# Transposing the first batch's q by DMA and searching the order of all operations anew, in a fused attention and convolution kernel

## Chip, cores and metric

The kernel runs on one core of one Trainium2 chip. The metric is device time in microseconds (us) of one execution, as the median over runs. A run counts as slow when it is over 1.5% above the fastest run of the same kernel in the same measurement.

## The reference, cut to what matters

```python
# q, k, v: (8 batches, 8 heads, 576, 64); w_phi: (64, 128)
def phi(x):
    proj = einsum('bhsd,df->bhsf', x, w_phi)
    proj = proj - max(abs(proj), axis=-1)
    return concatenate([exp(proj), exp(-proj)], axis=-1)
q_p, k_p = phi(q), phi(k)
kv  = einsum('bhsf,bhsd->bhfd', k_p, v);  z = sum(k_p, axis=2)
x   = einsum('bhsf,bhfd->bhsd', q_p, kv) / einsum('bhsf,bhf->bhs', q_p, z)
# then, with x as (8, 576, 512) and w_proj: (512, 1536)
x1, x2, x3 = split(x @ w_proj)
y   = x1 * irfft(rfft(x2) * rfft(filter)) * x3
out = y @ w_out
```

## The kernel before

The kernel is one long list of words, `PLAN`. Each word is a method with its arguments and, behind `@`, the PSUM bank it works in. Every engine and every queue executes its words in the order of the list, each as soon as its inputs are there.

```python
for word in PLAN.split():
    name, _, bank = word.partition("@")
    self.bank = int(bank) if bank else None
    f, *args = name.split(",")
    getattr(self, f)(*[int(a) if a.isdigit() else a for a in args])
```

These methods are the ones that the change and the argument touch (bodies cut to their instruction):

```python
def load(self, n, b):            # k, q or v of batch b: 576 KB, issued by GpSimd
    self.nc.gpsimd.dma_start(out=self.at(n + "n", b)..., in_=self.dram[n][b]...)
def trh(self, n, b, X):          # half of k or q transposed by DMA, issued by SP
    self.nc.sync.dma_start_transpose(out=self.at(n + "T", b)[:, 9*X:9*X+9, :], in_=...)
def T(self, n, b, X, i):         # the same by TensorE, 8 tiles (i=0) or 1 (i=1) into PSUM
    for k in range(8 * i, 8 + i):
        self.nc.tensor.transpose(..., self.at("ident"))
def Te(self, eng, n, b, X, i):   # and out of PSUM, by ACT or DVE
    self.copy(eng, self.at(n + "T", b)..., self.turned(m))
def trm(self, b):                # mT: the maxima of q, transposed by DMA, issued by SP
    self.nc.sync.dma_start_transpose(out=self.at("mT", b), in_=self.at("mh", b)...)
def fold(self, eng, b, odd):     # sum or difference of the halves of x: eo, what X2 reads
    self.port(eng, self.elem(eng).tensor_tensor(out=self.at("eo", b)..., in0=x..., in1=x..., op=op))
...
def port(self, eng, first, last=None):   # GpSimd waits for the DVE words ahead of it so marked
```

For a batch the words are: `Pk`, `Qn` (projections of k and q), `max*`, `ex` and `em` (maxima, exp), `vs` (products with v), `KV`, `trm` (mT), `Pq` (projection of q less its maximum), `NE`, `rc`, `xn` (numerator, division), `trx`, `trxt` (x transposed by DMA; `trxt` is its tail), `fold`, `X1`, `X2`, `X3` (x @ w_proj), `F` (the DFT), `m1` to `m3` (product with the filter's), `I` (back), `ym`, `O` (w_out), `st`. `H` and `filt_*` make the filter's DFT once; `warm` fills TensorE with multiplications of zeros.

Of the kernel before, what the change touches and what calls it, by code (L numbers as in the profile page):

```python
# [24 lines left out]
zeros loadh,k,0,1 w_load,phi gen_rows gen_cols,0 gen_cols,1 gen_turns,ACT,0 gen_angles,0 loadh,k,0,0  # L25
gen_ident warm,10,4@0 T,k,0,1,0@0 loadh,q,0,0 warm,1,4@1 warm,7,1@1 T,k,0,0,1@1 gen_turns,ACT,1
gen_angles,1 T,k,0,1,1@2 Te,DVE,k,0,1,1@2 loadh,q,0,1 T,k,0,0,0@3 Te,DVE,k,0,0,0@3 gen_selidx
gen_pads load,v,0 load,k,1 gen_sin,0 Te,DVE,k,0,0,1@1 w_phi,ACT warm,2,4@4 warm,3,1@4 T,q,0,0,1@4
Te,DVE,k,0,1,0@0 gen_sin,1 warm,5,4@5 warm,2,1@5 Pk,0,0@2 maxk,0,0@2 warm,1,4@1 warm,3,1@1 Pkt,0@0
ex,k,p,0,0@2 maxkt,0@0 exkt,m,0@0 Pk,0,1@6 gen_sel gen_selx Te,ACT,q,0,0,1@4 load,q,1 maxk,0,1@6  # L30
em,p,0,0 T,q,0,0,0@5 exkt,p,0@0 Te,DVE,q,0,0,0@5 warm,2,4@4 warm,1,1@4 Qn,0,1@4 ex,k,m,0,0@2
gen_five maxq,0,1@4 Pk,0,3@0 maxk,0,3@0 em,m,0,0 vs,POOL,m,0,0 T,q,0,1,1@2 Te,DVE,q,0,1,1@2
T,q,0,1,0@3 ex,k,m,0,1@6 Te,ACT,q,0,1,0@3 vs,POOL,p,0,0 ex,k,p,0,1@6 ex,k,p,0,3@0 ex,k,m,0,3@0
Qn,0,0@4 maxq,0,0@4 Pk,0,2@2 maxk,0,2@2 em,m,0,1 Qn,0,2@6 maxq,0,2@6 Qnt,0@4 maxqt,0@4 w_load,proj,1
ex,k,p,0,2@2 ex,k,m,0,2@2 em,p,0,1 Qn,0,3@0 maxq,0,3@0 mhi,0 vs,POOL,m,0,1 mlo,POOL,0 filt_load,SP,0
filt_load,SP,1 filt_fold,POOL,2 KV,0,0@6 load,k,2 trh,k,1,0 Pk,1,0@4 trh,k,1,1 Pk,1,1@2 maxk,1,0@4
ex,k,m,1,1@2 trh,q,1,1 warm,2,4@0 Qn,1,2@0 ex,k,m,1,0@4 KVe,DVE,0,0@6 trh,q,1,0 maxk,1,1@2
ex,k,p,1,0@4 Qn,1,3@6 ex,k,p,1,1@2 maxq,1,3@6 maxq,1,2@0 vs,POOL,p,0,1 trm,0 Pq,0,0@4 ex,q,m,0,0@4
load,v,1 Qn,1,1@6 maxq,1,1@6 ex,q,p,0,0@4 Pq,0,1@2 filt_fold,POOL,1 ex,q,m,0,1@2 Qnt,1@0 maxqt,1@0
ex,q,p,0,1@2 Qn,1,0@4 maxq,1,0@4 w_load,proj,0 NE,0,0@6 rc,0,0@6 xn,0,0@6 Pq,0,3@0 ex,q,m,0,3@0  # L40
ex,q,p,0,3@0 filt_fold,POOL,0 Pkt,1@2 maxkt,1@2 em,m,1,0 KV,0,1@4 KVe,DVE,0,1@4 NE,0,1@6 mhi,1
rc,0,1@6 exkt,m,1@2 mlo,POOL,1 vs,POOL,m,1,0 load,q,2 xn,0,1@6 gen_fwd5 Pqt,0@0 exqt,p,0@0
exkt,p,1@2 NE,0,3@4 rc,0,3@4 xn,0,3@4 exqt,m,0@0 Pk,1,3@6 maxk,1,3@6 Pq,0,2@4 ex,q,m,0,2@4 H,4@2
NEt,0@0 H_ev,DVE,4@2 rct,0@0 xnt,0,1@0 ex,q,p,0,2@4 xnt,0,0@0 gen_fwd ex,k,p,1,3@6 ex,k,m,1,3@6
warm,2,4@3 Pk,1,2@2 maxk,1,2@2 NE,0,2@4 rc,0,2@4 xn,0,2@4 ex,k,m,1,2@2 H,1@0 H_ev,DVE,3@0 em,p,1,0
ex,k,p,1,2@2 H_ev,DVE,1@0 trx,0,0 H,0@6 H_ev,DVE,2@6 H_ev,DVE,0@6 trh,k,2,0 vs,POOL,p,1,0 gen_inv
trm,1 Pq,1,1@4 ex,q,m,1,1@4 H_fix late load,q,3 trx,0,3 trx,0,1 ex,q,p,1,1@4 Pq,1,0@0 ex,q,p,1,0@0
warm,3,4@2 warm,2,1@2 KV,1,0@2 KVe,ACT,1,0@2 Pk,2,1@6 trx,0,2 X1,0,1@4 ex,q,m,1,0@0 fold,DVE,0,0
em,p,1,1 NE,1,1@2 fold,DVE,0,1 X1e,ACT,0,1@4 trxt,0 foldt,DVE,0,0 foldt,POOL,0,1 rc,1,1@2 xn,1,1@2
em,m,1,1 vs,POOL,m,1,1 X2,0,1@5 X2e,DVE,0,1@5 X2,0,2@0 X2e,DVE,0,2@0 Pk,2,0@2 ex,k,p,2,1@6 X2,0,4@4  # L50
X2e,DVE,0,4@4 ex,k,m,2,0@2 maxk,2,1@6 vs,POOL,p,1,1 X2e,ACT,0,5@4 X2,0,3@5 X2e,ACT,0,3@5 X2,0,0@0
X2e,DVE,0,0@0 w_load,proj,2 ex,k,p,2,0@2 trh,k,2,1 maxk,2,0@2 load,v,2 ex,k,m,2,1@6 X1,0,0@4
X1e,ACT,0,0@4 warm,2,1@1 F,0,0@0 m1,0,0@0 Pqt,1@6 exqt,p,1@6 exqt,m,1@6 NE,1,0@2 trh,q,2,1 rc,1,0@2
xn,1,0@2 F,0,1@4 Fe,ACT,0,0@0 X1t,0@6 X1te,ACT,0@6 m1,0,1@4 Pkt,2@2 exkt,m,2@2 exkt,p,2@2
Fe,ACT,0,1@4 warm,2,1@7 Qn,2,3@0 maxq,2,3@0 warm,2,1@7 KV,1,1@6 maxkt,2@2 trh,q,2,0 KVe,ACT,1,1@6
load,k,3 em,p,2,0 Qn,2,1@0 m2,POOL,0,1 Pq,1,3@2 ex,q,p,1,3@2 m3,POOL,0,1 m2,POOL,0,0 maxq,2,1@0
Qnt,2@4 maxqt,2@4 ex,q,m,1,3@2 F,0,4@6 m1,0,4@6 Pq,1,2@0 ex,q,p,1,2@0 Qn,2,2@4 maxq,2,2@4 X1,0,3@7
X1e,ACT,0,3@7 m3,POOL,0,0 ex,q,m,1,2@0 Qn,2,0@2 maxq,2,0@2 mhi,2 X1,0,2@6 trx,1,1 X1e,ACT,0,2@6
mlo,POOL,2 Pk,2,3@4 maxk,2,3@4 em,m,2,0 X3,0,1@7 tm,0,1@7 Pk,2,2@0 ex,k,m,2,2@0 load,q,4 NE,1,3@2
rc,1,3@2 xn,1,3@2 trx,1,0 trh,q,3,0 vs,POOL,p,2,0 vs,POOL,m,2,0 X3t,0@6 tmt,0@6 X3,0,0@7 tm,0,0@7  # L60
ex,k,m,2,3@4 ex,k,p,2,2@0 NE,1,2@2 rc,1,2@2 trh,q,3,1 xn,1,2@2 ex,k,p,2,3@4 I,0,1,0@6 Ie,0,1@6
maxk,2,2@0 X3,0,3@7 I,0,0,0@2 Ie,0,0@2 em,p,2,1 em,m,2,1 load,k,4 vs,POOL,m,2,1 tm,0,3@7 I,0,0,1@3
NEt,1@4 trm,2 Pq,2,0@0 ex,q,p,2,0@0 ex,q,m,2,0@0 rct,1@4 xnt,1,1@4 xnt,1,0@4 Pq,2,1@6 ex,q,p,2,1@6
I,0,1,1@2 Ip,0,1@2 Im,0,1@2 X3,0,2@4 vs,POOL,p,2,1 Ip,0,0@3 I,0,2,0@5 trx,1,3 Im,0,0@3 warm,3,1@2
Qn,3,0@0 maxq,3,0@0 Ie,0,2@5 trx,1,2 warm,3,1@2 KV,2,0@2 tm,0,2@4 w_load,out ex,q,m,2,1@6 Qn,3,3@0
maxq,3,3@0 KVe,ACT,2,0@2 trh,k,3,0 fold,DVE,1,0 I,0,3,0@5 Ie,0,3@5 Pq,2,2@6 ex,q,m,2,2@6 NE,2,0@2
rc,2,0@2 xn,2,0@2 Qn,3,1@4 maxq,3,1@4 KV,2,1@0 ex,q,p,2,2@6 KVe,ACT,2,1@0 ym,POOL,0,1 Pk,3,0@2
ex,k,p,3,0@2 ex,k,m,3,0@2 Qn,3,2@6 maxq,3,2@6 X2,1,0@0 X2e,ACT,1,0@0 NE,2,1@4 rc,2,1@4 xn,2,1@4
X2,1,1@1 X2e,ACT,1,1@1 maxk,3,0@2 fold,POOL,1,1 Pq,2,3@6 Qnt,3@4 I,0,3,1@0 ex,q,p,2,3@6 ym,POOL,0,0
trh,k,3,1 X2,1,2@1 ex,q,m,2,3@6 X2e,ACT,1,2@1 maxqt,3@4 X2,1,3@2 trxt,1 foldt,POOL,1,0 foldt,DVE,1,1  # L70
X2,1,4@3 Im,0,3@0 load,v,3 load,k,5 Ip,0,3@0 X2e,DVE,1,3@2 trx,2,0 X2e,ACT,1,5@3 X2e,ACT,1,4@3
Pqt,2@6 exqt,m,2@6 I,0,2,1@1 Ip,0,2@1 ym,POOL,0,3 Im,0,2@1 exqt,p,2@6 ym,POOL,0,2 NE,2,3@4 mhi,3
mlo,POOL,3 F,1,0@2 Pk,3,1@0 ex,k,p,3,1@0 rc,2,3@4 xn,2,3@4 F,1,1@6 Fe,ACT,1,1@6 Fe,DVE,1,0@2
m2,POOL,1,1 O,0,1@4 Oe,ACT,0,1@4 X1,1,0@5 X1e,ACT,1,0@5 m1,1,0@2 NEt,2@2 m1,1,1@6 rct,2@2 xnt,2,1@2
xnt,2,0@2 ex,k,m,3,1@0 X1,1,1@4 m2,POOL,1,0 X1e,ACT,1,1@4 X1,1,2@5 X1e,ACT,1,2@5 Pkt,3@2 exkt,m,3@2
exkt,p,3@2 maxk,3,1@0 NE,2,2@6 rc,2,2@6 X1t,1@4 X1te,ACT,1@4 O,0,2@5 Oe,ACT,0,2@5 load,q,5
m3,DVE,1,0 maxkt,3@2 xn,2,2@6 em,m,3,0 O,0,0@0 Oe,DVE,0,0@0 Pk,3,3@2 maxk,3,3@2 Pk,3,2@4 F,1,4@1
ex,k,m,3,2@4 m1,1,4@1 X3t,1@0 ex,k,p,3,2@4 maxk,3,2@4 tmt,1@0 O,0,3@6 X3,1,1@7 tm,1,1@7 m3,POOL,1,1
X3,1,0@1 em,p,3,0 trh,k,4,0 vs,POOL,m,3,0 trh,q,4,0 ex,k,p,3,3@2 vs,POOL,p,3,0 ex,k,m,3,3@2 tm,1,0@1
I,1,1,0@4 Ie,1,1@4 I,1,1,1@5 Ip,1,1@5 trx,2,1 em,m,3,1 st,0,1 I,1,0,0@0 Ie,1,0@0 trm,3 Pq,3,0@2  # L80
load,v,4 I,1,0,1@4 trx,2,3 ex,q,m,3,0@2 ex,q,p,3,0@2 em,p,3,1 trx,2,2 fold,DVE,2,1 X3,1,2@7 tm,1,2@7
Im,1,0@4 X1,1,3@0 X1e,ACT,1,3@0 fold,POOL,2,0 st,0,0 I,1,2,0@1 trxt,2 Ip,1,0@4 I,1,3,0@7 Ie,1,2@1
Im,1,1@5 ym,POOL,1,1 ym,POOL,1,0 vs,POOL,m,3,1 Ie,1,3@7 KV,3,0@2 KVe,ACT,3,0@2 Oe,DVE,0,3@6
trh,k,4,1 st,0,3 Qn,4,1@0 maxq,4,1@0 Pq,3,2@4 ex,q,m,3,2@4 ex,q,p,3,2@4 I,1,3,1@6 X3,1,3@7 NE,3,0@0
Im,1,3@6 Ip,1,3@6 Pk,4,0@2 foldt,POOL,2,1 ex,k,m,4,0@2 rc,3,0@0 xn,3,0@0 X2,2,0@6 Pk,4,1@0 tm,1,3@7
X2e,ACT,2,0@6 I,1,2,1@4 ex,k,m,4,1@0 maxk,4,0@2 Ip,1,2@4 ex,k,p,4,1@0 trh,q,4,1 X2,2,3@5
X2e,DVE,2,3@5 X1,2,0@6 X1e,ACT,2,0@6 maxk,4,1@0 Im,1,2@4 X2,2,1@7 foldt,POOL,2,0 ex,k,p,4,0@2
trh,k,5,1 X2,2,2@5 X2e,ACT,2,2@5 X2,2,4@6 X2e,ACT,2,4@6 X2e,ACT,2,5@6 X2e,DVE,2,1@7 Qn,4,0@0
maxq,4,0@0 Pq,3,1@2 ex,q,p,3,1@2 ex,q,m,3,1@2 vs,POOL,p,3,1 KV,3,1@4 KVe,DVE,3,1@4 Pkt,4@6 F,2,1@0
exkt,p,4@6 trx,3,0 Fe,ACT,2,1@0 trh,k,5,0 Qnt,4@4 maxqt,4@4 maxkt,4@6 F,2,0@2 m1,2,0@2 exkt,m,4@6  # L90
ym,POOL,1,2 ym,POOL,1,3 m1,2,1@0 X1t,2@4 X1te,ACT,2@4 O,1,0@5 Fe,ACT,2,0@2 Pq,3,3@6 ex,q,m,3,3@6
ex,q,p,3,3@6 X1,2,1@4 X1e,ACT,2,1@4 st,0,2 Oe,DVE,1,0@5 NE,3,2@0 load,q,6 rc,3,2@0 xn,3,2@0 NE,3,1@2
rc,3,1@2 xn,3,1@2 st,1,0 O,1,1@5 NE,3,3@6 m2,POOL,2,0 Oe,ACT,1,1@5 m3,POOL,2,0 Pqt,3@0 exqt,p,3@0
rc,3,3@6 xn,3,3@6 em,p,4,0 F,2,4@4 m1,2,4@4 trx,3,2 Pk,4,3@2 ex,k,m,4,3@2 Qn,4,2@6 maxq,4,2@6
maxk,4,3@2 exqt,m,3@0 X1,2,3@5 X1e,ACT,2,3@5 trx,3,3 X1,2,2@4 Qn,4,3@0 maxq,4,3@0 Pk,4,2@6
# [915 lines left out]
```

## Time and profile before

| | before |
|---|---|
| median of 3 runs | 322.75 us (322.12 to 323.13) |
| TensorE (PE) busy | 290.9 us, 90% of the profiled span of 323.1 |
| first projection of q (batch 0) | 19.1 us |
| first use of mT of batch 0 | 39.1 us |
| first X2 of batch 0 / of batch 1 | 62.8 / 98.8 us |
| first F of batch 1 | 106.9 us |

In all views PE is TensorE and PEld its weight loads, DVE, ACT, POOL and SP are VectorE, ScalarE, GpSimd and SyncE. The granted clock is the share of TensorE's full clock that its throttle let through. An eviction copies a result out of PSUM, the memory that TensorE writes to.

The profile is read in stretches of time, since the front (up to some 105 us, where the first batches fill the pipeline) waits for data and the rest is bound by TensorE. The prediction below shows the stretches, the chain of waits and the single waits.

### The profile page before, as it was taken

What the parts mean: (1) busy time and instruction counts of PE and PEld (TensorE: products, weight loads), DVE (VectorE), ACT (ScalarE), POOL (GpSimd) and SP (SyncE); (2) the same over time, 40 slices, a digit from 0 to 9 for tenths busy, and PEclk for the clock granted to TensorE, in tenths of its full rate; (3) what the DMA queues carried; (4) which work ended last, traced back from release to release, by engine and by line L of the source; (5) the groups of instructions that cost most, each with busy time, mean ns of one, the idle gap of its engine ahead of it and who ended that gap; (6) DMA issues with size and microseconds to landing.
All of it is one profiled execution on the core that took longest, in us unless ns stands there. A gap on an engine that the chain in (4) does not pass through costs nothing.

```text
span 323.1 us, 9519 instructions
## 1 busy us (share of the span) xinstructions
PE 290.9 (90%) x3959; PEld 164.2 (51%) x3959; DVE 247.5 (77%) x409; ACT 232.3 (72%) x366; POOL 222.3 (69%) x174
## 2 busy tenths in 40 slices
PE   6755387999879999999999999999999999999981
PEld 2433263555555556555645655565475554654430
DVE  4697389589885897879788887898779877767850
ACT  5697197789677787988788776887877787434532
POOL 8849933379965788879769698847868668812230
PEclk9587589799997999999999999999999999999997
DMA  6999999999999999755995557267953222331416
GB/s 125 224 190 151 179 191 142 158 129 186 185 135 131 173 170 172 176 91 136 102 227 110 129 101 136 17 108 131 154 131 82 63 68 42 75 92 33 97 37 160
DMA packets 78667, 41.52 MB, mean 129 GB/s; under 512 B 58976, under 2 KB 73440, under 8 KB 78624
## 3 DMA queue, kind: packets, MB, share of 16 engines
q1 hardware_dynamic: 63808, 24.66, 43.4%
q0 software_dynamic: 14816, 16.25, 35.5%
q8 instruction: 31, 0.51, 0.7%
q14 instruction: 12, 0.10, 0.1%
HBM read 33.75 MB, written 9.44 MB: 134 GB/s over the span
## 4 chain that ended last, share of the span: by engine, by line
PE 74%; DMA 13%; SPq 4%; POOL 3%; DVE 2%; issue 1%; ACT 1%; POOLq 0%; DVEq 0%; ACTq 0%
PE ps L846 17%; PE ps L938 9%; PE ps L803 8%; PE ps L897 7%; DMA mT<-mh 7%; PE ps L460 6%; PE ps L711 5%; PE ps L732 5%; SPq L550 4%; DMA kn<-in_k_dram 3%; PE ps L623 2%; PE ps L617 2%; DMA xTt<-xnt 2%; PE ps L589 2%; PE ps L596 2%; PE ps L853 2%
## 5 line engine op out<-in xcount | busy, mean ns | idle before, releaser
L846 PE MATMUL ps<-xT,wproj 128*128 128x512 bf16 x256 | 63.9, 379 | 0.0
L656 DVE TENSOR_REDUCE mq<-ps 128x8 f32<-128x1024 f32 (+1 forms) x40 | 44.0, 1113 | 17.0 <-PE ps L596 14.4
L915 POOL TENSOR_TENSOR yT<-cv,x1s 128x576 bf16<-128x576 f32 x27 | 34.6, 1288 | 29.0 <-DVE cv L905 17.3
L656 DVE TENSOR_REDUCE mk<-ps 128x8 f32<-128x1024 f32 (+1 forms) x40 | 44.3, 1112 | 6.8 <-PE ps L589 4.4
L696 POOL TENSOR_TENSOR vm<-vn,vm 128x1152 bf16<-128x1152 bf16 x16 | 34.4, 2150 | 13.4 <-ACT vm L690 11.4
L640 ACT ACTIVATE Eqm<-ps 128x1024 bf16<-128x1024 f32 x32 | 32.8, 1026 | 13.9 <-PE ps L623 10.0
L696 POOL TENSOR_TENSOR vp<-vn,vp 128x1152 bf16<-128x1152 bf16 x16 | 34.3, 2146 | 7.7 <-ACT vp L690 5.7
L834 POOL TENSOR_TENSOR t<-C,B 128x1024 bf16<-128x1024 bf16 x15 | 31.8, 2122 | 10.5 <-ACT C L716 9.6
L938 PE MATMUL ps<-wout,yT 128*128 128x512 bf16 x144 | 36.0, 379 | 0.8 <-DVE yT L915 0.8
L640 ACT ACTIVATE Ekm<-ps 128x1024 bf16<-128x1024 f32 x32 | 32.5, 1028 | 5.0 <-PE ps L589 4.4
L897 PE MATMUL ps<-inv,Y 128*128 128x288 bf16 (+1 forms) x192 | 35.7, 289 | 0.0
L640 ACT ACTIVATE Ekp<-ps 128x1024 bf16<-128x1024 f32 x32 | 32.5, 1029 | 3.9 <-DVE mk L656 2.6
L640 ACT ACTIVATE Eqp<-ps 128x1024 bf16<-128x1024 f32 x32 | 32.5, 1023 | 3.7 <-PE ps L623 3.6
L846 PEld LDWEIGHTS <-wproj 128*128 128x128 bf16 x256 | 23.1, 98 | 23.5 <-issue 0.2
L803 PE MATMUL ps<-wproj,eo 128*128 128x512 bf16 x128 | 31.8, 387 | 0.0
L905 DVE TENSOR_TENSOR cv<-es,ps 128x288 f32<-128x288 f32 x64 | 26.1, 447 | 6.8 <-ACT es L900 3.0
L829 DVE TENSOR_TENSOR Y<-ps,A 128x1024 bf16<-128x1024 f32 (+1 forms) x24 | 24.8, 1043 | 6.9 <-PE ps L460 2.8
L839 POOL TENSOR_TENSOR Y<-Y,t 128x1024 bf16<-128x1024 bf16 x12 | 25.5, 2121 | 5.6 <-DVE Y L839 3.6
L716 ACT COPY o<-ps 128x512 f32<-128x512 f32 x27 | 15.7, 587 | 13.7 <-PE ps L938 11.1
L883 DVE TENSOR_TENSOR x1s<-ps,x1s 128x512 bf16<-128x512 f32 x32 | 21.7, 685 | 4.4 <-PE ps L846 3.9
L716 ACT CAST x1s<-ps 128x512 bf16<-128x512 f32 (+1 forms) x34 | 18.7, 552 | 7.0 <-PE ps L846 4.0
L716 ACT CAST x2n<-ps 128x512 bf16<-128x512 f32 (+1 forms) x32 | 16.2, 520 | 9.9 <-PE ps L803 7.3
(150 smaller groups left out, 640.8 us busy)
## 6 DMA issues: line engine op xcount, KB each, us to landing
out_dram<-o SPq DMA_DIRECT2D x72, 128.0 KB, 2.4
vn<-in_v_dram POOLq DMA_DIRECT2D x8, 576.0 KB, 8.1
kn<-in_k_dram POOLq DMA_DIRECT2D x7, 576.0 KB, 9.2
qn<-in_q_dram POOLq DMA_DIRECT2D x7, 576.0 KB, 8.5
wproj<-in_moe_w_proj_dram POOLq DMA_DIRECT2D x3, 512.0 KB, 8.0
fl<-in_moe_filter_fft_dram SPq DMA_DIRECT2D x18, 64.0 KB, 5.3
kn<-in_k_dram POOLq DMA_DIRECT2D x2, 288.0 KB, 5.3
qn<-in_q_dram POOLq DMA_DIRECT2D x2, 288.0 KB, 8.2
```

The costliest lines, as they stand in the source:

```text
L640: self.nc.scalar.activation(e, self.db(), AF.Exp, bias=0.0, scale=1.0 if g == "p" else -1.0)
L656: self.nc.vector.tensor_reduce(out=out, in_=src, axis=AX.X, op=ALU.max, apply_absolute_value=True)
L696: self.port(eng, self.elem(eng).tensor_tensor(out=t[:, :, :, 0:64], in0=self.at("vn", b)[:, 2 * X:2 * X + 2], in1=t[:, :, :, 64:65].to_bro ...
L716: self.nc.scalar.copy(dst, src)
L803: self.mm(self.pb(0), eo[:, kt, 128 * c:128 * c + 128], w[:, kt, 512:1024], start=(kt == 0), stop=(kt == 3))
L834: self.port(eng, self.elem(eng).tensor_tensor(out=self.at("t2", b)[:, t, :], in0=self.at("C", b)[:, o, :], in1=self.at("B"), op=ALU.mult))
L839: self.port(eng, self.elem(eng).tensor_tensor(out=Y, in0=Y, in1=self.at("t2", b)[:, i:i + 3:2, :], op=ALU.add if i else ALU.subtract))
L846: self.mm(self.pb(0), w[:, kt, f0 + 128 * m:f0 + 128 * m + 128], x[:, kt, :], start=(kt == 0), stop=(kt == 3))
L897: self.mm(self.pb(0, 0, 288), y, t, start=(k == 0), stop=(k == 2))
L905: self.nc.vector.tensor_tensor(out=self.at("cv", 4 * b + m)[:, :, odd, :], in0=e, in1=o, op=ALU.subtract if odd else ALU.add)
L915: self.port(eng, self.elem(eng).tensor_tensor(out=self.at("yT", b)[:, m, 0:SEQ], in0=self.at("cv", 4 * b + m).rearrange("p j h t -> p (j h ...
L938: self.mm(self.pb(0), y[:, kt, 128 * j:128 * j + 128], w[:, kt, :], start=first and kt == ks[0], stop=last and kt == ks[-1])
```

## The change

The intent: q of batch 0 is transposed by two DMAs in place of 18 TensorE transposes and four evictions, and the order of every word and the engine of every eviction, product and sum is the result of a new search that used queue times as measured on the chip. Only `PLAN` differs. The core of the diff, with cuts marked:

```diff
-zeros loadh,k,0,1 w_load,phi gen_rows gen_cols,0 gen_cols,1 gen_turns,ACT,0 gen_angles,0 loadh,k,0,0
...
-em,p,0,0 T,q,0,0,0@5 exkt,p,0@0 Te,DVE,q,0,0,0@5 warm,2,4@4 warm,1,1@4 Qn,0,1@4 ex,k,m,0,0@2
-gen_five maxq,0,1@4 Pk,0,3@0 maxk,0,3@0 em,m,0,0 vs,POOL,m,0,0 T,q,0,1,1@2 Te,DVE,q,0,1,1@2
-T,q,0,1,0@3 ex,k,m,0,1@6 Te,ACT,q,0,1,0@3 vs,POOL,p,0,0 ex,k,p,0,1@6 ex,k,p,0,3@0 ex,k,m,0,3@0
...
+ex,k,m,0,0@2 ex,k,p,0,0@2 Pk,0,3@6 em,m,0,0 maxk,0,3@6 trh,q,0,0 ex,k,m,0,1@4 warm,1,4@0 warm,3,1@0
+Qn,0,1@0 ex,k,p,0,1@4 maxq,0,1@0 trh,q,0,1 Qnt,0@2 maxqt,0@2 Pk,0,2@0 maxk,0,2@0 em,m,0,1 Qn,0,3@2
...
+xn,0,1@0 trx,0,1 em,p,1,0 NE,0,2@4 rc,0,2@4 xn,0,2@4 trx,0,2 Pk,1,3@0 maxk,1,3@0 ex,k,m,1,2@2
+ex,k,p,1,2@2 trxt,0 Pkt,2@4 exkt,p,2@4 exkt,m,2@4 em,m,1,1 Qn,2,0@2 maxq,2,0@2 Qn,2,1@2 ex,q,m,0,3@6
...
+trh,k,3,0 Qn,2,2@2 NE,1,1@4 maxq,2,2@2 fold,POOL,0,0 Pq,1,3@0 rc,1,1@4 xn,1,1@4 trx,1,1 ex,q,m,1,2@6
+NE,1,0@2 rc,1,0@2 xn,1,0@2 ex,q,p,1,2@6 NE,1,2@6 rc,1,2@6 xn,1,2@6 X2,0,0@4 mhi,2 late X2e,DVE,0,0@4
...
```

The last two hunks show: on TensorE, batch 2's projections (`Qn,2`), and batch 1's `NE`, now come ahead of batch 0's first `X2`. In the old order `X2,0` came soon after the first `NE` of batch 1.

## The prediction

> **What bounds the kernel now.** I read the profile in this order: engine busy times, the 40 slices, busy time by stretch, the chain of waits, then single waits and the issue times on the queues.
>
> The first view is the busy time of each engine in stretches of time (columns: stretch, its length, busy time of PE, PEld, DVE, ACT and POOL with instruction counts, granted TensorE clock, DMA share, GB/s).
>
> ```profile
> 0.00:20.00 20.00, 13.87 (x100) 7.07 (x101) 12.84 (x40) 13.17 (x22) 13.71 (x28) 0.83 0.97 183
> 20.00:40.00 20.00, 9.27 (x171) 7.04 (x172) 12.64 (x13) 11.12 (x17) 19.25 (x15) 0.64 1.19 163
> 40.00:60.00 20.00, 15.82 (x265) 9.83 (x262) 17.99 (x34) 15.88 (x22) 6.57 (x6) 0.85 1.18 168
> 60.00:80.00 20.00, 19.80 (x346) 11.38 (x344) 15.62 (x20) 17.20 (x28) 14.79 (x10) 1.00 1.23 153
> 80.00:100.00 20.00, 17.27 (x337) 11.36 (x336) 15.34 (x25) 14.62 (x23) 16.18 (x12) 0.93 1.26 161
> 100.00:300.00 200.00, 199.15 (x2673) 110.95 (x2672) 163.04 (x262) 151.59 (x244) 147.60 (x101) 1.00 0.65 113
> 300.00:323.10 23.10, 15.75 (x82) 6.58 (x79) 10.05 (x19) 8.70 (x16) 4.24 (x4) 0.92 0.44 103
> ```
>
> From 100 to 300 us TensorE is busy 199.15 of 200 us at full clock: that part is bound by TensorE, and no new order can shorten it. DVE is at 82% there and ACT at 76%. All that an order can win lies in the first 100 us (TensorE 76.0 us busy, that is 24 us idle, much of the rest at a granted clock of 0.64 to 0.85) and in the tail of 23 us, of which some 7 are eviction and store latency.
>
> The chain of waits (start, length, what; in order of time) says where the first 100 us go:
>
> ```profile
> 9.59 11.21 DMA kn<-in_k_dram
> ...
> 24.88 1.34 SPq L550
> 26.27 5.70 SPq L550
> 32.07 6.95 DMA mT<-mh
> ...
> 48.41 8.49 DMA mT<-mh
> ...
> 81.26 6.42 DMA mT<-mh
> ```
>
> These are transposes by DMA on the one SP queue. mT holds the maxima of q, which the feature map of q needs: no exp of q before it. For batch 0 its input was ready at 27.9 us (the end of the subtraction that makes mh), but SP was still issuing four half transposes of k and q of batch 1 (L550, from 20.8 us). It was issued at 32.07 and landed at 39.06. The quickest landing of any mT is 2.3 us. Batches 1 and 2 meet the same at 48.4 and 81.3 us. The waits by engine (total, times, longest, in the first 100 us) tell what that costs:
>
> ```profile
> PE ps L623 <- DMA mT<-mh: 8.0, 3, 4.3
> PE ps L596 <- DMA qT<-qn: 3.9, 1, 3.9
> ...
> ACT Eqm L640 <- PE ps L623: 7.8, 2, 7.2
> ```
>
> The idle TensorE is then clocked down, so the matmuls after a wait run slowly. The work that these waits hold back is ACT's (exp, 1.03 us for each 128x1024, eight a batch for q and eight for k) and DVE's (maximum, 1.22 us, half as many). The first projection of batch 0 starts only at 61.4 us.
>
> **What the Trainium skill says.** (1) "TensorE: Matmul & The Clock Gate", Part 1: the array runs at half rate until it has been busy for some 3.4 us, and goes back after an idle window. This trace agrees: 0.64 granted from 20 to 40 us, and the transposes of k take 271 ns against 223 for those of q. (2) "DMA: Bandwidth & Descriptors", Issuing engines are not separate DMA queues: DMAs of all issuers run on the same 16 engines. Agrees: the DMA slices read 9 almost without a break until 112 us, and a half transpose lands in 4.3 us (k) or 7.7 us (q), against a fastest of 2.8. (3) "Advanced Engine Details and Errata", X-Bar Transpose (TRN2): transposing DMAs are as fast as ordinary ones. The half load of q (288 KB) takes 8.2 us here and the half transpose of the same size 7.7, so nothing contradicts it; the cost is a place in the line, not the transposition.
>
> **The change, part by part.**
>
> *Removed:* 18 TensorE transposes of q. In the timeline they take 0.29 + 0.62 + 0.66 = 1.6 us in the first 21 us, where TensorE waits anyway. Their evictions are 1.00 + 0.27 us on ACT and 0.68 + 0.21 on DVE. Worth under 1 us on the path. *Added:* two half transposes of q by DMA at the head of the SP queue. q lands at about 13 to 14 us (issued at 4.5 and 5.3, some 8 us to landing), so with 4 to 5 us each (the four of before took (39.06 - 20.8)/4 = 4.6, mT included) the halves are there at about 18.5 and 22 us. Today the first q projection runs at 19.1 and the half of the last heads at 24.8. So this part alone is about even; it buys DVE and ACT time at the start for DMA time.
>
> *Engines:* counting the words of the two orders with the durations of the rows, the sums are ACT 253 against 255 us, DVE 262 against 264, TensorE's needed work 261 against 260, POOL 225 against 209 (these add overlapping latencies, so they stand 6 to 9% above the busy times). Work moves from POOL to DVE (two products, two sums and a fold of some 2.12 us each that cost DVE about 0.68), nothing is saved. Filling matmuls drop from 58 to 34. So a gain must come from waits.
>
> *Order, mT of batch 0:* before it SP now has six half transposes (q0, q0, q1, q1, k1, k1) and nine loads of the filter, but starts at about 14 instead of 20.8 us. 14 + 6 x 4.3 = 40 us, less what fewer competing loads give (the first part of w_proj and v of batch 1 now come later). I expect its landing at 37 to 41 us against 39.06: little gained. DVE and ACT have about as much behind them then (DVE 30 against 28, ACT 23.5 against 23 in sums). Gain 0 to 3 us, I take 1.5.
>
> *Order, mT of batches 1 and 2:* in the old order mT(1) stands behind a transpose of xn and one of k, and its use follows at once. In the new it is issued right after batch 0's first division, and between it and its use stand three more projections of q for batch 2, two for k of batch 1, all divisions of batch 0 and the sums of KV. mT(2) is issued before the first DFT of batch 0 and used after it and three projections. Today these cost TensorE 2.7 and 1.0 us of idleness, 1.6 us of filling, ACT 3.1 us before an exp of q. Most should go: 3 us.
>
> *Order, the rest:* a further 1.7 us of TensorE idle at 94.8 us and the clock of 0.87 from 90 to 100 us: 1 us. When batch 0 reaches its first X2, the new order has done NE of three parts of batch 1, all its Pq, and k and q of batch 2 partly; the old reaches the same TensorE sum (24 us) one X2 round later, at 66.4 us. ACT and DVE sums there are 2 to 4 us higher in the new, which takes back part: already netted in the above. *Tail:* 16 of the 20 last matmuls of w_out follow the last product, today 17; the ring of three output tiles still makes two evictions wait for a store. No change; the risk of 0.5 us either way. Shorter idleness also raises the clock earlier: 0.5 us.
>
> Sum: 0.8 + 1.5 + 3 + 1 + 0.5 = 6.8 us, so 322.75 - 6.8 = 316.0.
>
> **Rivals.** *ACT and DVE are the true bound of the front.* From 40 to 80 us they are busy 33.1 and 33.6 of 40 us; as all of that work stays, removing waits for mT moves the idleness elsewhere. For it: the sums above; against it: between 20 and 40 us both idle over 7 us, mostly for mT. It would give 319 to 322. *The DMA engines are the bound:* their slices are at 9 until 112 us, and the change adds two half transposes to them. Then mT(0) lands at 43 or later and the time is 321 to 325. Against it: the time in which a DMA is busy includes waiting in line, and up to 227 GB/s are moved in one slice against a mean of 161 here. *The search got it right:* it knew the queues' times, so mT(0) lands near 30 us and ACT no longer has its 7.2 us hole; with the 3 + 1 us above that gives 308 to 312.
>
> **Range and chances.** The second rival is unlikely, since an order that was searched with measured queues should not lose. The first and third are about equally likely and pull apart, so the range is wide: 309.5 to 321.5. The 2% line is at 316.3, next to my middle: faster 0.50, same 0.45, slower 0.05.
>
> **What would show it.** Right: TensorE idle for mT under 2 us in all; TensorE busy in the first 60 us above today's 39 us, or the same needed work in less; first X2 of batch 0 no later than 65 us with NE of batch 1 begun before; 100 to 300 us unchanged at over 99%. Wrong in the step of mT(0): landing after 42 us, or before 33. Wrong as a whole: if TensorE has new holes beyond 100 us, or DVE, which takes on POOL's work, is above 90% there and holds TensorE up.

## The result, and the profile after

The changed kernel took 341.92 us in the median of 4 runs (335.49 to 344.85), of which two count as slow; the kernel before took 322.94 beside it. The ratio is 1.046, with a 95% interval of 1.031 to 1.061: slower. Ratios here are the mean time of one kernel's fast runs over that of the other's in the same rounds, so not quite the ratio of the medians. Measured again as e0, the unchanged kernel gave 1.058 (1.047 to 1.070).

The busy times by stretch of the changed kernel (columns: stretch, its length, busy time of PE, PEld, DVE, ACT and POOL with instruction counts, granted TensorE clock, DMA share, GB/s):

```profile
0.00:20.00 20.00, 11.17 (x73) 4.73 (x73) 15.76 (x43) 14.32 (x22) 12.39 (x29) 0.85 0.98 171
20.00:40.00 20.00, 8.21 (x164) 6.43 (x166) 11.82 (x12) 8.64 (x14) 10.02 (x7) 0.55 1.06 176
40.00:60.00 20.00, 9.77 (x214) 7.47 (x211) 11.52 (x18) 11.92 (x17) 10.23 (x9) 0.71 1.23 182
60.00:80.00 20.00, 14.80 (x314) 9.64 (x311) 14.66 (x23) 13.84 (x21) 14.24 (x12) 0.84 1.08 132
80.00:100.00 20.00, 18.22 (x172) 8.65 (x171) 14.28 (x21) 16.80 (x28) 3.17 (x5) 0.94 1.28 184
100.00:300.00 200.00, 198.61 (x2830) 112.72 (x2830) 166.69 (x269) 152.78 (x243) 147.94 (x99) 1.00 0.64 112
```

(The DMA share is the summed time of the packets over that of 16 engines; packets overlap, so it can pass 1.) From 100 to 300 us hardly anything changed. From 20 to 80 us, taken together, every engine is less busy than before, TensorE with 8.21, 9.77 and 14.80 us in place of 9.27, 15.82 and 19.80, at a lower granted clock. No engine became the bound; all wait more.

The chain of waits of the changed kernel (start, length, what):

```profile
5.27 8.18 DMA qn<-in_q_dram
13.47 1.81 SPq L548
15.38 7.49 SPq L548
...
36.69 7.76 DMA mT<-mh
...
54.21 5.60 DMA qT<-qn
...
74.97 3.43 issue
...
89.03 9.85 DMA xT<-xn
99.62 0.68 DVE eo L785
...
118.02 2.37 PE ps L458 x12
```

q of batch 0 has landed by 13.47 us and its transposes are issued at once, but issuing the second keeps SP (L548) until 22.9 us, and the two halves land only at 26.9 and 27.9 us. mT of batch 0 is issued at 36.69 and lands at 44.45 (before: 32.07 and 39.02). The later waits for mT are gone from the chain, and waits for qT and xT stand in their place. The last line is the first F of batch 1: it comes 11 us later than before, where the same view has

```profile
107.04 1.18 PE ps L460 x6
```

That line settles where the loss lies. The last matmuls of TensorE are in the timeline (start, length, what; before first)

```profile
312.74 3.86 PE L938 MATMUL ps<-wout,yT 128*128 128x512 bf16 x17 [0.85 <-DVE yT L915]
...
323.53 3.31 PE L936 MATMUL ps<-wout,yT 128*128 128x512 bf16 x14 [0.35 <-DVE yT L913]
```

so they end at 316.6 and 326.8 us. From this F (in the timeline: 106.88 us before, 117.86 after) to that end it is 209.7 us before and 209.0 after. The whole loss of the profiled run, 11 us, lies ahead of it.

And it isn't more work. These are TensorE's busy time up to that F and, in the second line of each pair, the part of it that is filling (`warm`); before first:

```profile
0.00:106.88 106.88, 82.88 (x1286) 50.46 (x1287) 79.03 (x139) 77.14 (x115) 73.69 (x74) 0.86 1.16 163
...
0.00:106.88 106.88, 14.77 (x58) 5.69 (x58) 0.86 1.16 163
```

```profile
0.00:117.86 117.86, 78.81 (x1241) 47.25 (x1242) 84.12 (x140) 78.28 (x120) 65.69 (x71) 0.81 1.06 163
...
0.00:117.86 117.86, 10.64 (x34) 3.53 (x34) 0.81 1.06 163
```

82.88 - 14.77 = 68.1 us before, 78.81 - 10.64 = 68.2 us after: the needed work is the same, and it takes 11 us longer to get through. In the four stretches of 20 us up to 80 us (the same views, filling taken off) TensorE is busy with needed work for 1.4, 0.6, 3.8 and 4.6 us less than before: most of the lag arises from 40 to 80 us, after q of batch 0 is there. The waits of TensorE in those 117.86 us (total, times, longest):

```profile
PE ps L594 <- DMA qT<-qn: 9.9, 2, 9.1
PE ps L601 <- DMA kT<-kn: 3.8, 2, 3.1
PE ps L594 <- DVE mq L654: 3.6, 3, 1.4
PE ps L621 <- DMA mT<-mh: 3.5, 1, 3.5
...
PE ps L801 <- DVE Y L827: 2.7, 1, 2.7
```

The wait for mT fell from 8.0 to 3.5 us, as the change meant it to. But qT rose from 3.9 to 9.9, and kT (3.8), the maxima (3.6, before 0.2) and DVE (2.7) are new.

### The profile page after: what moved, and what is told of

Read it like the earlier page. It is cut to its first block, busy times and chain, and to the rows that moved or that the text cites.

```text
span 333.7 us, 9450 instructions
## 1 busy us (share of the span) xinstructions
PE 287.3 (86%) x3917; PEld 161.4 (48%) x3917; DVE 251.2 (75%) x414; ACT 232.7 (70%) x367; POOL 206.5 (62%) x164
## 4 chain that ended last, share of the span: by engine, by line
PE 72%; DMA 10%; SPq 7%; DVE 3%; ACT 2%; issue 2%; POOL 1%; DVEq 0%; POOLq 0%; ACTq 0%
PE ps L844 16%; PE ps L895 9%; PE ps L801 8%; PE ps L936 8%; PE ps L458 6%; SPq L548 6%; PE ps L730 5%; PE ps L709 5%; DMA xT<-xn 3%; DMA qn<-in_q_dram 2%; DMA mT<-mh 2%; PE ps L615 2%; PE ps L587 2%; PE ps L594 2%; PE ps L621 2%
## 5 line engine op out<-in xcount | busy, mean ns | idle before, releaser
L694 POOL TENSOR_TENSOR vm<-vn,vm 128x1152 bf16<-128x1152 bf16 x16 | 34.4, 2154 | 32.1 <-DVE eo L785 17.3
L913 POOL TENSOR_TENSOR yT<-cv,x1s 128x576 bf16<-128x576 f32 x26 | 33.0, 1278 | 19.1 <-DVE cv L903 10.1
L832 POOL TENSOR_TENSOR t<-C,B 128x1024 bf16<-128x1024 bf16 x13 | 27.6, 2123 | 20.0 <-ACT C L714 17.7
L594 PE MATMUL ps<-wphi,qT 64*128 64x128 bf16 x256 | 15.2, 242 | 14.4 <-DMA qT<-qn 9.9
L714 ACT COPY o<-ps 128x512 f32<-128x512 f32 x30 | 17.8, 593 | 13.9 <-PE ps L936 11.3
L714 ACT CAST x2n<-ps 128x512 bf16<-128x512 f32 (+1 forms) x34 | 17.1, 503 | 12.1 <-PE ps L801 9.7
L730 PE MATMUL ps<-KVs,Eqm 128*128 128x65 bf16 x256 | 20.7, 197 | 3.4 <-issue 3.4
```

Of the source, the lines that this page charges most:

```text
L694: self.port(eng, self.elem(eng).tensor_tensor(out=t[:, :, :, 0:64], in0=self.at("vn", b)[:, 2 * X:2 * X + 2], in1=t[:, :, :, 64:65].to_bro ...
L714: self.nc.scalar.copy(dst, src)
L730: self.mm(self.pb(u, c, c + 65), E.rearrange("f i t -> f (i t)"), KVs[:, u, v, s, :], start=(s == 0), stop=(s == 1))
L832: self.port(eng, self.elem(eng).tensor_tensor(out=self.at("t2", b)[:, t, :], in0=self.at("C", b)[:, o, :], in1=self.at("B"), op=ALU.mult))
L913: self.port(eng, self.elem(eng).tensor_tensor(out=self.at("yT", b)[:, m, 0:SEQ], in0=self.at("cv", 4 * b + m).rearrange("p j h t -> p (j h ...
```

## The experiments

Eighteen runs, all with correct results, each timed in 3 rounds. Nine of them change the new order a little, one the old one a little, two are the kernel itself or the part undone, and six join the two orders or move larger pieces.

One regularity holds through them. In 19 of the 20 profiles (these and the two of above) the time from the first F of batch 1 to the end of TensorE's last matmul is 208.6 to 209.7 us (e11: 213.2). (The expectation of e15 calls it 205.8 us, which is the time to the start of the last group of matmuls.) So the start of that F is the time of the kernel less a constant, and it is given with each run as F1. Landmarks in the tables are of the profiled run, which was slow in e1, e2, e5, e15 and e16; no conclusion rests on those alone.

### Is it the transposes of q? e0, e1, e2, e3

e0 is the changed kernel once more. e1 keeps the new order and gives q of batch 0 back to TensorE; e2 keeps the old order and takes q by DMA; e3 is the changed kernel with the loads behind q held back.

```diff
 e1 (new order)
-trh,q,0,0   -trh,q,0,1
+T,q,0,0,1@1 Te,ACT,q,0,0,1@1 T,q,0,0,0@0 Te,DVE,q,0,0,0@0        (behind maxk,0,3)
+T,q,0,1,1@3 Te,DVE,q,0,1,1@3 T,q,0,1,0@2 Te,ACT,q,0,1,0@2        (behind maxq,0,1)
 e2 (old order)
-T,q,0,*  -Te,*,q,0,*
+filt_load,SP,0 filt_load,SP,1 trh,q,0,0 trh,q,0,1                (the filter's loads moved ahead)
 e3 (new order)
+  load,q,1 waits for the maximum of part 3 of k (about 18.5 us); load,k,1 and load,v,0, moved
+  up beside it, and load,k,2 come behind it on the same engine
```

Expected of e0:

> The changed kernel unchanged, on the same chip as the other three. All theories: 335 to 345 us. It tells how wide its own runs spread (335.5 to 344.9 in the first four) next to those of the kernel before.

Of e1:

> The changed kernel with its own order, but q of batch 0 transposed by TensorE again (18 transposes and 4 evictions put in where q lands). Theory A (the two half transposes of q stood in the DMA line behind 2.3 MB of loads and held everything back): first q projection at 16 to 20 us instead of 27, mT of batch 0 lands by 40 us instead of 44.5, time 325 to 331 us. Theory B (the rest of the new order lost the time, the transposes are harmless): first q projection early too, but the time stays at 335 to 342 us.

Of e2:

> The kernel before with its own order, only q of batch 0 transposed by DMA (the filter's loads stay ahead of it on SP, where they in fact ran). Theory A: the halves take over 8 us to land, first q projection at 23 us or later instead of 19.1, time 326 to 332 us. Theory B: 321 to 325 us, as before.

Of e3:

> The changed kernel with the loads of q1, k1, v0 and k2 held back until the fourth part's maximum of k is taken (about 18 us, today issued at 8.2 to 11 us). Theory A: with the DMA engines free, both halves of q land within 6 us of their issue (by 20 us instead of 27) and the first q projection runs by 20 us; the time gains little or nothing since batch 1 now comes late: 328 to 338 us. If the halves still take over 10 us, the loads are not what they stood behind, and theory A falls.

| | median (range), us | ratio to before | first projection of q | mT(0) used | F1 |
|---|---|---|---|---|---|
| before (same rounds) | 323.34 (317.37 to 325.73) | 1 | 19.1 | 39.1 | 106.9 |
| e0 | 338.32 (336.28 to 349.74) | 1.058 (1.047 to 1.070) | 26.9 | 44.0 | 120.1 |
| e1 | 343.88 (336.84 to 345.03) | one fast run, 336.84 | 20.1 | 40.5 | 126.6 |
| e2 | 339.18 (330.07 to 342.97) | one fast run, 330.07 | 27.3 | 48.7 | 125.7 |
| e3 | 341.49 (341.33 to 345.87) | 1.075 (1.059 to 1.091) | 17.6 | 50.4 | 123.3 |

Over the mean of the three fast runs of before, 319.0 us, the two single fast runs are 1.056 (e1) and 1.035 (e2), worked out by hand and without an interval.

Two things follow. The half transposes wait for the loads beside them: the two queues of the changed kernel from 13 to 18.5 us (packets, MB, share of 16 engines), and the issue line of the two halves (how many, median us to landing), read

```profile
q0 software_dynamic: 975, 1.09, 115.4%
q1 hardware_dynamic: 154, 0.04, 5.3%
...
qT<-qn SPq DMA_TRANSPOSE x2, 13.0
```

and the same stretch of e3, where no load is under way, reads

```profile
q1 hardware_dynamic: 2368, 0.59, 47.5%
...
qT<-qn SPq DMA_TRANSPOSE x2, 2.9
```

Four loads issued by GpSimd between 8.2 and 11.7 us (q and k of batch 1, v of batch 0, k of batch 2) take the engines, and the transposes get 0.04 of 1.13 MB. Without them a half takes 2.9 us in place of 13.0. This cause of q's late start is shown. But it is not the whole loss: e1 has q at 20.1 us and is as slow as e0, and e3 has it at 17.6 us and is slower, because the held loads bring batch 1 late (TensorE waits 13.1 us for its qT) and mT of batch 0 behind it on SP.

So in the old order the new way to transpose q loses some 3.5% by itself (one fast run), and in the new order undoing it wins nothing (again one fast run). The two parts of the change don't add up: each of them alone reads slower than the kernel before.

### Is it the bursts of loads? e5 to e8

In the changed kernel v, v, k and q of batches 2 to 4 are issued together at about 80 us, and the transposes of x of batch 1 then take 9.85 us (the chain above). e5 moves three of these loads behind the products of batch 2; e6 is e5 with q by TensorE; e7 and e8 also part the first burst, with q by TensorE and by DMA.

```diff
 e5
+vs,POOL,m,2,0 load,v,3 load,k,4 load,q,4         (the loads from their places further up)
 e6 = e5 with the edit of e1
 e7 = e6 and
+vs,POOL,p,0,1 load,q,2
+filt_fold,POOL,0 load,k,3 w_load,proj,1
+trm,0 filt_load,SP,0
 e8 = e7 without the edit of e1
```

Expected of e5, e6, e7 and e8:

> The changed kernel, only three loads (v3, k4, q4), which it issues together with v2 at 80 to 83 us, put behind the first product of batch 2 on GpSimd, which waits for the fold of batch 1. Theory A2 (transposes on the SP queue starve behind bursts of loads on the GpSimd queue, wherever the order makes a burst): the last transposes of xn of batch 1 land within 5 us instead of 9.9, the fold of batch 1 and its X2 come 5 to 8 us earlier, time 328 to 333 us. Theory B2 (the order loses elsewhere, the burst is chance): 336 to 342 us.

> The same with q of batch 0 by TensorE as well: both places mended. Theory A2: in the run with q by TensorE alone the gain at the start was eaten at the second burst (16 us for the transposes of xn), so with both mended the two gains add: 320 to 327 us. If it stays over 333 us, something else in the new order sets its time.

> As the last, and in addition the burst of four loads around the first mT (q2 at 35.7, v1, k3 and part of w_proj at 40.8 to 43 us) taken apart: q2 behind two products, k3 and w_proj behind the folding of the filter, and the second half of the filter's loads behind mT on SP. Theory A2: mT of batch 0 lands by 37 us, q2's transposes no longer wait, time 312 to 322 us, below the kernel before. Theory B2: no better than the last.

> All the loads spread as in the last, but q of batch 0 by DMA as in the change. With the last, the changed kernel and the one with q by TensorE alone it makes a two by two. Theory A2: the transposes of q still stand behind the loads of q1, k1 and v0, so it is 5 to 12 us slower than the last: 322 to 332 us. If it is equal to the last, the move of q to DMA costs nothing by itself.

| | median (range), us | ratio to before | mT(0) used | F1 |
|---|---|---|---|---|
| before (same rounds) | 321.53 (319.72 to 333.95) | 1 | | |
| e5 | 349.23 (344.3 to 357.25) | 1.081 (1.062 to 1.099) | 44.2 | 139.1 |
| e6 | 347.28 (344.81 to 349.6) | 1.083 (1.072 to 1.094) | 39.0 | 127.8 |
| e7 | 345.04 (342.99 to 346.91) | 1.076 (1.065 to 1.086) | 36.6 | 124.6 |
| e8 | 349.24 (347.94 to 350.25) | 1.089 (1.083 to 1.095) | 40.7 | 131.3 |

None came near the 312 to 333 us that the theory of the bursts (A2) foretold for them. All four read slower than the changed kernel (1.046 and 1.058 in other rounds; the interval of e7 overlaps that of e0). e6 shows one reason in one line, the longest wait of its TensorE between 60 and 140 us (the X2 of the tail of batch 1, for the sum of that tail):

```profile
PE ps L807 <- POOL eo L794: 11.8, 1, 11.8
```

The SP queue is executed in order. With the load of k of batch 4 moved back, its transpose waits for the load at the head of SP, and the transpose of batch 1's tail, which needs nothing more, stands behind it: it is issued at 108.6 us. e5, e7 and e8 carry the same wait (11.4, 9.5 and 11.2 us), so these four are no clean trial of the bursts; e9 and e11 below are. e7 and e8, which differ in the transposes of q alone, are 4.2 us apart in the mean of their fast runs (5 to 12 were expected); e5 and e6, which do too, are level. mT(0) at 36.6 us in e7, the earliest of all, brought nothing in the end: what is gained there is lost later.

### Is it the place on the SP queue? e9 to e12

e9 is e6 with the tail of batch 1 moved to right behind its last part. e10 takes e1 and puts batch 0's last part and its tail ahead of k and q of batch 2 on SP; e11 is both; e12 is e10 with q by DMA.

```diff
 e9 = e6 and
+trx,1,3 trxt,1
 e10 = e1 and
+ex,q,p,0,3@6 ex,q,m,0,3@6
+trx,0,2 NE,0,3@6 rc,0,3@6 xn,0,3@6 trx,0,3
+trxt,0 trh,k,2,0 trh,k,2,1 trh,q,2,0 trh,q,2,1
 e11 = e10 with e5 and e9;   e12 = e10 without the edit of e1
```

Expected of e9 to e12:

> The kernel with q by TensorE and the second burst split, with one more move: the transposes of batch 1's tail (xTt) ahead of the transposes of k of batch 4 on the SP queue. In the run before they waited on SP behind a transpose whose load had just been put later, and TensorE stood 11.8 us for the fold that needs them. Theory C (what costs is the order on the in-order SP queue: a transpose that is needed now stands behind one that is needed later or not yet loaded): that wait goes, 332 to 338 us. Theory A2 (bursts alone) would expect nothing more: 343 to 349 us.

> The new order with q of batch 0 by TensorE, and batch 0 finished first: the last NE of batch 0 and all four transposes of its xn go ahead of the transposes of k and q of batch 2 on SP and ahead of the projections of batch 2 on TensorE. Nothing else is moved. Theory C: fold of batch 0 by 61 us instead of about 70 to 73, first X2 by 64 us, time 326 to 336 us. Theory A2: no gain, since the loads are where they were: 337 to 345 us.

> Both of these together with the second burst split. Theory C: the gains add, 316 to 328 us, around the kernel before. If it stays above 335 us, theory C is not the main term either.

> Batch 0 first as above, with q of batch 0 by DMA as in the change. Theory C with A as a second term: 6 to 12 us slower than the same with q by TensorE, as the first q projection is at 27 us again. If the two are equal, the transposes of q cost nothing once the order is mended.

| | median (range), us | ratio to before | first X2 of batch 0 | F1 |
|---|---|---|---|---|
| before (same rounds) | 323.28 (321.91 to 326.18) | 1 | 62.8 | 106.9 |
| e9 | 339.27 (338.45 to 341.98) | 1.050 (1.039 to 1.061) | 82.0 | 121.8 |
| e10 | 337.34 (334.65 to 340.45) | 1.040 (1.029 to 1.051) | 83.7 | 121.2 |
| e11 | 339.82 (336.05 to 342.7) | 1.046 (1.035 to 1.057) | 81.8 | 117.5 |
| e12 | 342.10 (339.67 to 344.99) | 1.055 (1.045 to 1.065) | 83.2 | 122.1 |

SP in e6 and, last line, in e9 (start, length, what):

```profile
106.48 2.02 SPq L550 DMA_TRANSPOSE kT<-kn  x1
108.59 1.40 SPq L775 DMA_TRANSPOSE xTt<-xnt  x1
...
94.69 1.17 SPq L775 DMA_TRANSPOSE xTt<-xnt  x1
```

e9 confirms the head of the queue: the tail is issued at 94.7 us, the wait of 11.8 us is gone, and the time falls from 1.083 (e6, other rounds) to 1.050 of before, 8 us between the medians and 10 by the ratios; 332 to 338 us were expected. With the wait gone, the split of the second burst still wins nothing: e9 is at 1.050 where e1 without it had 1.056 (one fast run), and e11 at 1.046 where e10 has 1.040. So theory A2 falls. e10 and e12 differ in the transposes of q alone: 1.040 against 1.055, so these cost some 4.8 us of the median there (6 to 12 were expected), though the intervals still overlap. e10 also has a miss: the four parts of x of batch 0 are issued by 56.3 us, and the first X2 of batch 0, foretold by 64 us, comes at 83.7. In the list it still stands behind the words of batches 1 and 2. e11 decides on theory C (the order on SP): it was to give 316 to 328 us, and to fall as the main term above 335. It took 339.8.

### Which stretch of the order loses? e13 to e15

Here the two orders are joined. e13 has the words of the old order up to the end of the filter (some 60 us) and then the rest in the new order; e14 has the new order, with q by TensorE, up to the first X2 of batch 0 and then the old; e15 has the old order up to the first X2 of batch 1 (99 us) and then the new. Readers of a bank that the cut left open were taken along.

Expected of e13, e14 and e15:

> The order of the kernel before, q of batch 0 by TensorE, up to the end of the filter (some 60 us), all that is left in the order of the changed kernel. If the new order loses in its first 60 us (theory A): 320 to 326 us, F of batch 1 starting by 112 us. If it loses between 60 and 107 us, by holding X2 of batch 0 behind projections of batch 2 whose q and k are still being transposed (theory B): 332 to 342 us, TensorE idle for qT or kT for over 6 us between 60 and 85 us, first X2 of batch 0 after 72 us.

> The order of the changed kernel with q of batch 0 by TensorE up to its first X2 of batch 0, all that is left in the order of the kernel before. Under A and under B alike the loss is in the front, so F of batch 1 comes after 115 us and the time is 332 to 342 us. If the loss came only after the first X2 of batch 0 (theory C: loads of v, k and q in one burst at 80 us), it would be 320 to 328 us.

> The order of the kernel before up to the first X2 of batch 1 (some 99 us), then the order of the changed kernel. If the new order is as good as the old from there on, as the equal 205.8 us from F of batch 1 to the end say: 320 to 326 us, F of batch 1 by 110 us. If its later part also loses: over 328 us. A gain over the kernel before (under 319 us) is not expected.

| | median (range), us | ratio to before | first X2 of batch 0 | of batch 1 | F1 |
|---|---|---|---|---|---|
| before (same rounds) | 320.78 (318.73 to 323.61) | 1 | 62.8 | 98.8 | 106.9 |
| e13 | 335.31 (333.79 to 336.68) | 1.047 (1.039 to 1.054) | 75.6 | 99.3 | 118.1 |
| e14 | 340.99 (339.0 to 342.71) | 1.065 (1.058 to 1.072) | 82.0 | 118.9 | 125.8 |
| e15 | 331.62 (326.93 to 333.57) | 1.027 (1.016 to 1.038) | 62.8 | 103.4 | 115.8 |

Theory A, that the new order loses in its first 60 us, would have made e13 as fast as before; it falls as the only cause. e13 is level with the old order until 60 us (q at 18.5, mT(0) at 38.8) and then loses nearly as much as the whole change. Its two stretches after that are

```profile
60.00:80.00 20.00, 14.20 (x244) 10.13 (x238) 13.00 (x18) 11.12 (x16) 13.39 (x13) 0.66 1.07 127
80.00:100.00 20.00, 14.40 (x145) 7.20 (x146) 12.92 (x20) 13.60 (x25) 1.19 (x1) 0.93 1.24 191
```

against 19.80 and 17.27 us of TensorE before. But theory B, that X2 stands behind batch 2's qT and kT, had foretold 6 us of idleness for these, and there is none between 60 and 85 us. What its TensorE waits for there is GpSimd's product for batch 1's KV (2.8 us) and the maxima (1.4), and from 60 to 80 us it runs at a clock of 0.66. e15 has a miss too: 320 to 326 us were expected, and the joint at 99 us costs 2.7% as well, all of it ahead of F1. e14 fell in the range that both theories gave it. A joined order is one that nobody searched, so part of a loss after a joint may be the joint's own: these runs narrow the place down, and don't prove it.

### What in that stretch? e16, e17, e18

e16 changes e10: batch 2's projections of q and of the tail of k, their maxima and mT go behind X2 of batch 0, and the sums of batch 0 go to DVE. e18 does the same to e13, with one part of k of batch 2 as well, and leaves the sums. e17 changes e13 the other way about: batch 0's x out at once, its sums on DVE, and its X2 ahead of KV of batch 1 and all of batch 2, as in the old order.

```diff
 e16 = e10 and
+X2e,ACT,0,4@1 Pkt,2 exkt,*,2 maxkt,2 Qn,2,* maxq,2,* Qnt,2 maxqt,2 mhi,2 mlo,POOL,2 trm,2
-fold,POOL,0,*   +fold,DVE,0,0 fold,DVE,0,1                   (behind NE,1,1)
 e17 = e13 and
+trx,0,2 trxt,0 trh,k,2,1 trh,q,2,0 trh,q,2,1
+fold,DVE,0,* foldt,DVE,0,* X2,0,0 X2,0,1 X2,0,2 X2,0,3 X2,0,4 (each with its eviction)
 e18 = e13 and
+X2e,ACT,0,4@1 Pkt,2 ... Qnt,2 maxqt,2 mhi,2 mlo,POOL,2 trm,2 Pk,2,3 maxk,2,3 ex,k,*,2,3
```

Expected of e16, e17 and e18:

> e10 with the projections of q of batch 2 and of the tail of its k, their maxima and mT moved behind X2 of batch 0, and the sum and difference of batch 0 on DVE in place of GpSimd. Under B the first X2 of batch 0 starts at 68 to 75 us in place of 84, and the time falls from e10's 337 to 325 to 332 us. If something else holds that X2 (the filter, or ACT's exps of batch 1), it still starts after 78 us and the time stays at 334 to 340.

> e13 with one thing changed: the last transposes of batch 0's x issued at once, its sum and difference on DVE, and X2 of batch 0 placed ahead of KV of batch 1 and of all of batch 2 on TensorE, as the kernel before has it. If the new order loses by leaving TensorE nothing to do while batch 1's products (exp, product on GpSimd) are made: first X2 at 62 to 67 us, F of batch 1 by 113 us in place of 118, 325 to 331 us against e13's 335. If the place of X2 doesn't matter: 333 to 338, F of batch 1 after 116 us.

> e13 with only the projections of batch 2 (q, the tail and one part of k), their maxima and mT moved behind X2 of batch 0 on TensorE; batch 1's KV and NE stay ahead of it. If batch 2's place is the cause (theory B): first X2 by 70 us and 325 to 331 us. If batch 1's KV is what holds it: the first X2 comes at 71 us or later, and the time is 332 us or more, since batch 2 is then late as in e16.

| | median (range), us | ratio to before | first X2 of batch 0 | of batch 1 | F1 |
|---|---|---|---|---|---|
| e16 | 351.36 (347.5 to 353.44) | 1.089 (1.080 to 1.099) | 80.5 | 117.0 | 135.7 |
| before (beside e17, e18) | 322.41 (318.97 to 325.04) | 1 | 62.8 | 98.8 | 106.9 |
| e17 | 336.25 (334.47 to 338.53) | 1.047 (1.038 to 1.055) | 59.6 | 100.4 | 119.8 |
| e18 | 343.65 (343.01 to 344.36) | 1.069 (1.061 to 1.077) | 71.1 | 107.7 | 126.3 |

e16 was measured in the rounds of e13 to e15. None of them regains anything. e16 was made badly for its purpose: one part of k of batch 2 stayed ahead of X2 while its transpose had moved back, and TensorE waited 10.8 us for it. e18 is clean, and speaks against batch 2's place as the cause: X2 comes at 71.1 us, TensorE waits 7.0 us for the product of batch 1 on GpSimd, and batch 2 is then late. e17 brings X2 of batch 0 to 59.6 us, earlier than in the kernel before, and the time is e13's all the same. Its TensorE, in the timeline (start, length, engine and line, what, in brackets how long it sat idle before and for what):

```profile
59.56 3.84 PE L803 MATMUL ps<-wproj,eo 128*128 128x512 bf16 x15 [1.61 <-ACT Eqm L640]
...
64.98 0.40 PE L596 MATMUL ps<-wphi,qT 64*128 64x128 bf16 x8
66.70 0.40 PE L596 MATMUL ps<-wphi,qT 64*128 64x128 bf16 x8 [1.31 <-DVE mq L656]
71.97 0.61 PE L596 MATMUL ps<-wphi,qT 64*128 64x128 bf16 x8 [4.87 <-DMA qT<-qn]
```

X2 is done by 64 us, and then TensorE goes into batch 2's projections and stands 4.9 us for their q. It looks as if the work that used to bridge such waits has only moved ahead of them; that was not tested. The theory of e17 (X2's place alone) falls too.

## Why the prediction was wrong

It said 316.0 us with 309.5 to 321.5, and 0.05 for slower by over 2%; the kernel took 341.9.

- *Right: the bound beyond 100 us and the tail.* TensorE is busy 198.61 of 200 us from 100 to 300 us, and from the first F of batch 1 to the end of its last matmul both kernels need 209 to 210 us.
- *Right as to the wait, wrong as to the gain: "mT of batches 1 and 2 ... Most should go: 3 us".* TensorE's waits for these two, 2.7 and 1.0 us, are gone; the 3.5 us left are batch 0's. But other waits took their place, and no time was won.
- *Wrong: "with 4 to 5 us each ... the halves are there at about 18.5 and 22 us. ... this part alone is about even".* They landed at 26.9 and 27.9 us, 13 us after issue, and the first projection of q came at 27.0 in place of 19.1 us. The 4.6 us each are the pace of a queue later in the old order, when mostly one or two loads were under way; here four loads of 576 KB were. e3 shows it: 2.9 us without them. The trace of before had a hint that was read only half: the same text notes 7.7 us for a half of q, and 8.2 us for a load issued beside others. What it costs the kernel is less sure: e12 against e10 and e8 against e7 say 4 to 5 us, e2 3.5% of the old order (one fast run), e0 against e1 and e5 against e6 nothing.
- *Wrong in size: "I expect its landing at 37 to 41 us".* It landed at 44.45, beyond the 42 us that the text itself named as the sign of this step being wrong. The six halves were not what made it late: they were all there by 34.1 us, ahead of the sum's 40. Behind them SP issued the nine loads of the filter (32.3 to 36.6 us), which the sum names and gives no time, and mT then took 7.8 us to land, with a load of q issued 1 us before it. e6 and e7 show both terms: e7 moves these loads behind mT, which then goes from issue to landing in 2.2 us (30.2 to 32.4) in place of 5.1 (33.9 to 39.0).
- *The step that failed most: the sum.* It took the waits of the old order that the new one removes as won. All it set against them is 2 to 4 us more of ACT and DVE work, "already netted in the above". What was not looked for are waits that the new order makes: qT + 6.0, kT + 3.8, maxima + 3.4, DVE + 2.7 us on TensorE. The 1.7 us of idleness at 94.8 us, counted as won in part, has gone, but a wait of the same kind ("issue") of 3.4 us stands at 75 us. The needed work ahead of F1 is 68.1 us of a front of 107 us in the old order; the rest is waiting and filling, so a front has far more room to lose than the 6.8 us that the sum found to win.
- *The rival "The DMA engines are the bound"* foretold mT(0) "at 43 or later", which came true, though not through the two added halves, and gave it 321 to 325 us. It was called unlikely "since an order that was searched with measured queues should not lose". That is trust in where a change comes from and no reading of the trace; it is also what put 0.05 on slower.
- *"first X2 of batch 0 no later than 65 us"*: it came at 79 us. By the prediction's own tests (TensorE idle for mT under 2 us, over 39 us busy in the first 60) the profile called it wrong: 3.5 and 29.2 us.
- *A slip without weight:* the prediction reads the DMA slices of the kernel before as 9 until 112 us; on its profile page they are 9 until 129 us.

What is shown: the loss lies ahead of F1; it is waiting and not work; the late q comes from loads that share the DMA engines; a transpose that waits for its load holds up others behind it on SP. What is not settled: which property of the old order ahead of F1, most likely between 60 and 107 us, makes it better. Moving batch 2's projections, batch 0's X2, its x on SP, or the loads, each by itself, won little or nothing back: the best of these, e10, is still at 1.040, and the larger joins of e13 and e15 lose at either cut. No run moved all of them together as the old order has them. Nor is it known why the search preferred the new order. That it used queue times which no longer held once its own order had moved the loads is only argued. GpSimd stands 17.3 us for DVE's sum of batch 1 in the changed kernel and 16 to 25 us in others of the new order; that wait was not tried alone. The trace limits it: in these 17.3 us (83.2 to 100.4) TensorE is busy 15.05 us at full clock, so there it costs TensorE at most 2.2 us at once.

TensorE's 3.4 us of "issue" at 75 us have a likely cause in the traces. They end 1.3 us after a packet of 16 KB on the queue that the profile calls instruction (q8, 76.2 to 77.1 us). The same holds for all 14 waits for "issue" of over 1.2 us that TensorE has in the 20 profiles, that at 94.8 us of the kernel before among them: such a packet ends 1.2 to 1.6 us ahead of the end of the wait, though there are only some 30 of them in a whole execution. So TensorE seems to have run out of instructions there. How long the wait is differs from order to order (1.7 us before, 3.4 after, 5.6 in e9). No run tried it.

## What to carry to other kernels

An order for engines that wait in line is worth what its whole pattern of arrivals is worth: removing the waits that the chain shows tells what can be won at most, not what will be, and the new order's own waits have to be looked for before a sum is made. Before moving work to DMA, count the bytes that are queued when it will be issued; a quiet duration from elsewhere in the trace is not its duration there. And find the point from which two kernels take the same time: here the start of one matmul group told the time of 19 of 20 profiled runs within a microsecond or so, and made each trial readable.

## What the Trainium skill lacked or had wrong

- "Advanced Engine Details and Errata", X-Bar Transpose (TRN2), says that transposing DMAs are as fast as ordinary ones and expects 350 to 400 GB/s. With no load beside them the half transposes of q took 2.9 us, at 283 to 294 GB/s in the busy slices of e3, under that figure. Beside four loads issued by GpSimd the same took 13.0 us. The page has no word on the second case, which is the one that made q late here.
- "DMA: Bandwidth & Descriptors", Queues, rings and completion order, says that each engine goes round its queues packet by packet. From 15.4 to 18.5 us, when the first half was wholly issued and both queues had work, the queue of the loads moved 528 packets of the profile (0.59 MB) and that of the transposes 154 (0.04 MB): neither the packets nor the bytes were shared evenly. Later, from 18.5 to 27 us, it was 999 against 2007 packets (1.11 and 0.51 MB). Whether the profile's packets are those of the page isn't known, so this doesn't refute it; but the page gives no way to foretell such shares.
- No page puts a figure on a queue whose head waits for its input. In e6 a transpose that was ready stood behind one whose load had not landed, and cost TensorE 11.8 us; with the two exchanged (e9) the kernel was 8 to 10 us faster.
